# The general path of a fused hash attention and MLP kernel, written as loops over query tiles and row tiles

## The chip, the cores and the metric

The kernel runs on one core of one Trainium2 chip. The metric is device time in microseconds (us); the kernel before was run three times and took 315.37 us in the median (315.19 to 315.73). The profiled execution is a further run of the same kernel.

## What is computed

Attention in which a query sees only those keys that fall in the same hash bucket, then layer norm and a two-layer MLP with a residual.

```python
q_bits = (np.einsum('bhsd,dk->bhsk', q, proj) > 0)      # 6 bits; k_bits alike
mask = q_bucket[:, :, :, None] == k_bucket[:, :, None, :]
scores = scale * np.matmul(q, k.transpose(0, 1, 3, 2))
scores = np.where(mask, scores, -1000000000.0)
scores = scores - np.max(scores, axis=-1, keepdims=True)
attn = np.exp(scores)
attn = attn / (np.sum(attn, axis=-1, keepdims=True) + 1e-09)
x = np.matmul(attn, v)            # then heads side by side: (4, 768, 512)
xn = (x - mu) / np.sqrt(var + 1e-06) * g_ln
out = x + np.maximum(xn @ w_ch1, 0.0) @ w_ch2
```

There are 4 batches, 8 heads, 768 positions and 64 channels a head; q, k and v are normal draws times 0.1. w_ch1 is 512 x 2048, w_ch2 is 2048 x 512.

## The kernel before

The kernel has two paths for the same computation.

**The main path** (all of `tile_hash_attn__then__metaformer_identity_kernel` up to line 901) exponentiates scores without subtracting their maximum first, with the mask folded into the scores as extra rows. It walks through 12 chunks of 256 query rows. For each, attention units (scores on TensorE, the exponential on ScalarE at L456, products with the values at L480) are interleaved with the MLP of the chunk before it (L577 up, L618 and L600 down), by an order written out by hand. The MLP of the last chunk closes the main path: its last row tile is computed in two halves of 256 columns. For each half VectorE adds the residual (L604) and ScalarE's DMA queue stores it (L608). The chunk's other row tile was stored by SyncE's queue (L627).

**The general path** (`general_path`) is exact for scores of any size. It is there for inputs with which the shortcut is not safe. In chunk 10, `safety` computes a flag from the largest squared norms of q and k (L687). After the main path's last work every engine reads that flag into a register (L902) and branches on it (L903): the general path runs when the flag is 0. With these inputs the flag is 1, and no engine runs the general path.

**How the program lies in memory.** Each engine has an instruction stream of its own, in four parts that follow each other: the main path, which ends in the flag's read and the branch; the general path; a short *skip block*, to which the branch goes when the general path isn't wanted; and the *end block*. The skip block exists since the general path would have raised semaphores: each engine waits until its own semaphore has the main path's final value, and then adds what the general path would have added (L903). SyncE does so for those DMA semaphores that the general path uses. The end block (L1080, in the launch code at the file's end) is the same on every run: SyncE waits for 12 semaphores or pairs of them, which cover all DMA queues and all engines; then come a barrier of all five engines, the clearing of the semaphores by GpSimd, and a second barrier. On VectorE the skip block and the end block are six instructions: the semaphore update, a jump, a drain, a wait for the first barrier, a drain, a wait for the second.

SyncE's skip block before has eight semaphore updates, DMAHW0 to DMAHW7, in this order. DMAHW5 and DMAHW6 are the semaphores of the last two stores of the main path (L608). Its twelve waits in the end block name DMAHW5, DMAHW6 and DMAHW7 last.

Of the kernel before, what the change touches and what calls it, by code (L numbers as in the profile page):

```python
# [9 lines left out]
F32 = mybir.dt.float32  # L10
BF16 = mybir.dt.bfloat16
# [897 lines left out]
def general_path(tc, q, k, v, proj1, gbc, n_bits, w1_sb, w2_sb, identf, ident, out):  # L909

    nc = tc.nc
    P = 128
    B, H, S, D = q.shape
    ND, NH = w1_sb.shape[1], w2_sb.shape[1]
    d_model = w2_sb.shape[2]
    NC = S // P
    scale = 1.0 / math.sqrt(D)
    with ExitStack() as ctx:
# [7 lines left out]
        xd = dram.tile([B * H, S, D], F32, name="xd")  # L926
        with tc.For_i(0, B * H, 1) as i:
            nat = {}
            for nm, src in (("q", q), ("k", k), ("v", v)):
                t = pool.tile([P, NC, D], F32, tag=f"g{nm}", name=f"g{nm}")  # L930
                nc.sync.dma_start(
                    out=t,
                    in_=src.rearrange("b h (p c) d -> (b h) p c d", p=P)[
                        bass.ds(i, 1)
                    ].rearrange("o p c d -> (o p) c d"),
                )
                nat[nm] = t
            vb = pool.tile([P, NC, D], BF16, tag="gvb", name="gvb")
            nc.vector.tensor_copy(vb, nat["v"])
            tb, bits = {}, {}  # L940
            for nm in "qk":
                tf = pool.tile([D, S], F32, tag=f"gT{nm}", name=f"gT{nm}")
                for c in range(NC):
                    tp = psp.tile([D, P], F32, tag="gtp", name="gtp")
                    nc.tensor.transpose(tp, nat[nm][:, c, :], identf)
                    nc.vector.tensor_copy(tf[:, c * P : (c + 1) * P], tp)
                tb[nm] = pool.tile([D, S], BF16, tag=f"gb{nm}", name=f"gb{nm}")
                nc.vector.tensor_copy(tb[nm], tf)
                bits[nm] = pool.tile([n_bits, S], BF16, tag=f"gbit{nm}", name=f"gbit{nm}")
                for s0 in range(0, S, S // 2):  # L950
                    hp = psp.tile([n_bits, S // 2], F32, tag="ghp", name="ghp")
                    nc.tensor.matmul(
                        hp, proj1[0:D, 0:n_bits], tf[:, s0 : s0 + S // 2]
                    )
                    nc.vector.tensor_scalar(
                        bits[nm][:, s0 : s0 + S // 2], hp,
                        scalar1=0.0, scalar2=0.5, op0=AOP.is_gt, op1=AOP.subtract,
                    )
            for c in range(NC):
                s = pool.tile([P, S], F32, tag="gs", name="gs")  # L960
                hit = pool.tile([P, S], F32, tag="ghit", name="ghit")
                for s0 in range(0, S, S // 2):
                    sl = slice(s0, s0 + S // 2)
                    bp = psp.tile([P, S // 2], F32, tag="gbp", name="gbp")
                    nc.tensor.matmul(bp, bits["q"][:, c * P : (c + 1) * P], bits["k"][:, sl])

                    nc.vector.tensor_scalar(
                        hit[:, sl], bp, scalar1=n_bits / 4 - 0.25, scalar2=None,
                        op0=AOP.is_gt,
                    )  # L970
                    sp = psp.tile([P, S // 2], F32, tag="gsp", name="gsp")
                    nc.tensor.matmul(sp, tb["q"][:, c * P : (c + 1) * P], tb["k"][:, sl])
                    nc.vector.tensor_scalar_mul(s[:, sl], sp, scale)
                nc.vector.tensor_mul(s, s, hit)
                nc.vector.tensor_scalar(
                    hit, hit, scalar1=1e9, scalar2=1e9, op0=AOP.mult, op1=AOP.subtract
                )
                nc.vector.tensor_add(s, s, hit)
                mx = pool.tile([P, 1], F32, tag="gmx", name="gmx")
                nc.vector.reduce_max(mx, s, axis=AX.X)  # L980
                nc.vector.tensor_scalar(
                    s, s, scalar1=mx, scalar2=None, op0=AOP.subtract
                )
                pb = pool.tile([P, S], BF16, tag="gpb", name="gpb")
                nc.scalar.activation(pb, s, AF.Exp)
                den = pool.tile([P, 1], F32, tag="gden", name="gden")
                nc.vector.reduce_sum(den, pb, axis=AX.X)
                nc.vector.tensor_scalar_add(den, den, 1e-9)
                nc.vector.reciprocal(den, den)
                op = psp.tile([P, D], F32, tag="gop", name="gop")  # L990
                for kj in range(NC):
                    pt_p = psp.tile([P, P], BF16, tag="gpt", name="gpt")
                    nc.tensor.transpose(pt_p, pb[:, kj * P : (kj + 1) * P], ident)
                    pt = pool.tile([P, P], BF16, tag="gpts", name="gpts")
                    nc.vector.tensor_copy(pt, pt_p)
                    nc.tensor.matmul(
                        op, pt, vb[:, kj, :], start=(kj == 0), stop=(kj == NC - 1)
                    )
                xo = pool.tile([P, D], F32, tag="gxo", name="gxo")
                nc.vector.tensor_scalar_mul(xo, op, den)  # L1000
                nc.sync.dma_start(
                    out=xd.rearrange("i (p c) d -> i p c d", p=P)[bass.ds(i, 1), :, c, :]
                    .rearrange("o p d -> (o p) d"),
                    in_=xo,
                )
        xv = xd.rearrange("(b h) (p c) d -> b c p h d", b=B, p=P)
        ov = out.rearrange("b (p c) d -> b c p d", p=P)
        with tc.For_i(0, B, 1) as b:
            for c in range(NC):
                x = pool.tile([P, d_model], F32, tag="gx", name="gx")  # L1010
                nc.sync.dma_start(
                    out=x.rearrange("p (h d) -> p h d", h=H),
                    in_=xv[bass.ds(b, 1), c].rearrange("o p h d -> (o p) h d"),
                )
                stats = pool.tile([P, 6], F32, tag="gst", name="gst")
                mv = pool.tile([P, 2], F32, tag="gmv", name="gmv")
                nc.vector.bn_stats(stats, x)
                nc.vector.bn_aggr(mv, stats)
                rs = pool.tile([P, 1], F32, tag="grs", name="grs")
                mh = pool.tile([P, 1], F32, tag="gmh", name="gmh")  # L1020
                nc.vector.memset(mh, -0.5)
                nc.vector.tensor_scalar_add(rs, mv[:, 1:2], 1e-6)
                nc.gpsimd.tensor_tensor(rs, rs, mh, op=AOP.pow)
                xn = pool.tile([P, d_model], BF16, tag="gxn", name="gxn")
                nc.vector.scalar_tensor_tensor(
                    xn, x, mv[:, 0:1], gbc, op0=AOP.subtract, op1=AOP.mult
                )
                xnT = pool.tile([P, ND, P], BF16, tag="gxnT", name="gxnT")
                for dt in range(ND):
                    tp = psp.tile([P, P], BF16, tag="gpt", name="gxp")  # L1030
                    nc.tensor.transpose(tp, xn[:, dt * P : (dt + 1) * P], ident)
                    nc.vector.tensor_copy(xnT[:, dt, :], tp)
                hb = pool.tile([P, NH, P], BF16, tag="ghb", name="ghb")
                for nt in range(NH):
                    hp = psp.tile([P, P], F32, tag="gsp", name="ghh")
                    for dt in range(ND):
                        nc.tensor.matmul(
                            hp, w1_sb[:, dt, nt * P : (nt + 1) * P], xnT[:, dt, :],
                            start=(dt == 0), stop=(dt == ND - 1),
                        )  # L1040
                    nc.vector.tensor_scalar_max(hb[:, nt, :], hp, 0.0)
                o2 = psp.tile([P, d_model], F32, tag="gop", name="go2")
                for nt in range(NH):
                    nc.tensor.matmul(
                        o2, hb[:, nt, :], w2_sb[:, nt, :],
                        start=(nt == 0), stop=(nt == NH - 1),
                    )
                res = pool.tile([P, d_model], F32, tag="gres", name="gres")
                nc.vector.scalar_tensor_tensor(
                    res, o2, rs, x, op0=AOP.mult, op1=AOP.add  # L1050
                )
                nc.sync.dma_start(
                    out=ov[bass.ds(b, 1), c].rearrange("o p d -> (o p) d"), in_=res
                )


# [28 lines left out]
```

## Time and profile before

| quantity | value |
|---|---|
| median of three runs | 315.37 us (315.19 to 315.73) |
| the profiled execution's own time | 316.02 us |
| its span, from the first to the last instruction of the program | 314.5 us |
| granted TensorE clock over the span | 0.997 |
| TensorE matmuls, busy | 301.7 us (96% of the span) |
| VectorE, ScalarE, GpSimd busy | 185.7, 217.3, 84.4 us |
| HBM traffic | 27.98 MB read, 6.88 MB written |

The profile calls the engines PE (TensorE; PEld are its weight loads), DVE (VectorE), ACT (ScalarE), POOL (GpSimd) and SP (SyncE). A trailing q, as in DVEq, marks instructions that the engine's sequencer carries out itself: branches, semaphore waits and updates, register loads, drains. They are not counted as busy. In the views of one source line a row gives the engine, the instruction, its count, shortest/median/longest duration in ns, and the start of the first and the last in us from the span's start. In the list of DMA queues a row gives packets, megabytes, and the time that the packets took as a share of 16 engines over the window; the queues called "instruction" bring the engines' own code. A row of the table by stretches gives the stretch, its length, each engine's busy time, the granted clock, the share of 16 DMA engines that was busy, and GB/s.

### The profile page before, as it was taken

The numbers are of one execution on the slowest core, as the hardware profiler recorded it, in microseconds if no ns is written. First come the engines' busy times: TensorE is split into PE (matmuls) and PEld (weight loads), VectorE is DVE, ScalarE is ACT, GpSimd is POOL, SyncE is SP. The second block draws the span as 40 slices with busy tenths as digits, with TensorE's granted clock in tenths as the row PEclk, the third lists the DMA queues.
The fourth block names the chain that finished last, engine by engine and source line by source line (L and its number), as shares of the span: only waits on it lengthen the run. The fifth ranks groups of instructions, "written<-read, shape, count | busy, mean of one in ns | idle before, by whom it ended". The sixth has DMA issues, their size and how long they took to land.

```text
span 314.5 us, 7839 instructions
## 1 busy us (share of the span) xinstructions
PE 301.7 (96%) x3268; PEld 226.6 (72%) x3268; DVE 185.7 (59%) x404; ACT 217.3 (69%) x272; POOL 84.4 (27%) x110
## 2 busy tenths in 40 slices
PE   7979999999999999999999999999999999999991
PEld 6556788678679679678678679679688688686661
DVE  1799996653765755744774783743734645456320
ACT  5676977776798778687798777778798577663110
POOL 3467540914320127150470650100100100101000
PEclk9999999999999999999999999999999999999998
DMA  7999998377396467685198655230200210200302
GB/s 249 361 198 302 208 340 121 101 119 186 57 329 136 102 224 139 170 270 142 36 249 157 160 110 120 45 81 2 66 36 2 67 35 2 67 35 2 101 1 76
DMA packets 64971, 40.94 MB, mean 130 GB/s; under 512 B 47153, under 2 KB 59953, under 8 KB 64929
## 3 DMA queue, kind: packets, MB, share of 16 engines
q1 hardware_dynamic: 60224, 31.59, 39.9%
q0 software_dynamic: 4128, 8.13, 11.0%
q10 hardware_dynamic: 576, 0.66, 0.6%
q8 instruction: 27, 0.44, 0.6%
q14 instruction: 16, 0.12, 0.1%
HBM read 27.98 MB, written 6.88 MB: 111 GB/s over the span
## 4 chain that ended last, share of the span: by engine, by line
PE 83%; DVE 10%; ACT 2%; issue 1%; DMA 1%; POOL 0%; ACTq 0%; SPq 0%; POOLq 0%
PE hp L577 25%; PE o L618 23%; PE sc L446 17%; PE av L480 10%; PE hash L321 3%; DVE slots L238 2%; DVE slots L262 2%; PE tpose L200 1%; PE wakep L762 1%; DVE bt L287 1%; PE o L600 1%; PE hash L252 1%; DMA xnT<-xn 1%; DVE xn L529 1%; DVE x L508 1%
## 5 line engine op out<-in xcount | busy, mean ns | idle before, releaser
L456 ACT ACTIVATE ex<-sc,expb 128x1024 bf16<-128x1024 f32 x144 | 159.6, 1113 | 56.5 <-PE sc L446 54.5
L577 PE MATMUL hp<-xnT,w_sb 128*128 128x256 bf16 x768 | 98.7, 272 | 1.7 <-DVE hbuf L587 1.0
L618 PE MATMUL o<-w_sb,hbuf 128*128 128x512 bf16 x368 | 92.9, 379 | 0.0
L446 PE MATMUL sc<-slots 70*128 70x256 bf16 x576 | 86.7, 272 | 2.1 <-POOL slots L238 1.1
L577 PEld LDWEIGHTS <-w_sb 128*128 128x128 bf16 x768 | 72.0, 97 | 11.2 <-issue 2.5
L480 PEld LDWEIGHTS <-ex 128*128 128x128 bf16 x1152 | 54.0, 98 | 15.7 <-ACT ex L456 1.6
L446 PEld LDWEIGHTS <-slots 70*128 70x128 bf16 x576 | 51.8, 97 | 17.5 <-issue 4.5
L480 PE MATMUL av<-vaug,ex 128*128 128x65 bf16 x1152 | 58.8, 194 | 0.3 <-ACT ex L456 0.2
L587 DVE TENSOR_SCALAR hbuf<-hp 128x512 bf16<-128x512 f32 x48 | 32.8, 684 | 43.2 <-PE hp L577 42.0
L618 PEld LDWEIGHTS <-hbuf 128*128 128x128 bf16 x368 | 33.7, 97 | 25.5
L540 POOL TENSOR_SCALAR rs<-mv 128x2 f32<-128x2 f32 x12 | 9.1, 759 | 157.7 <-DVE mv L528 157.7
L589 ACT ACTIVATE hbuf<-hp 128x512 bf16<-128x512 f32 x48 | 28.5, 594 | 20.2 <-PE hp L577 20.2
L623 DVE SCALAR_TENSOR_TENSOR x<-o,rs,x 128x512 f32<-128x512 f32 x23 | 17.1, 744 | 26.3 <-PE o L618 23.4
L529 DVE SCALAR_TENSOR_TENSOR xn<-x,mv,gbc 128x512 bf16<-128x512 f32 x24 | 17.9, 751 | 0.8
L508 DVE TENSOR_TENSOR x<-x,rc 128x256 f32<-128x256 f32 x36 | 17.1, 476 | 1.2
L500 DVE TENSOR_SCALAR rc<-av 128x4 f32<-128x4 f32 x36 | 5.7, 157 | 19.8 <-PE av L480 19.8
L527 DVE BATCH_NORM_STATS2 stats<-x 128x6 f32<-128x512 f32 x24 | 16.5, 690 | 0.4
L351 POOL CAST vaug<-vnat 128x1536 bf16<-128x1536 f32 x8 | 12.1, 1509 | 13.4 <-DMA vnat<-in_v_dram 13.4
L501 DVE TENSOR_TENSOR x<-av,vsum 128x256 f32<-128x256 f32 x36 | 14.9, 414 | 0.0
L180 ACT ACTIVATE knat<-knat 128x768 f32<-128x768 f32 x16 | 13.4, 836 | 0.0
L180 ACT ACTIVATE qnat<-qnat 128x768 f32<-128x768 f32 x16 | 13.3, 833 | 0.0
L282 POOL CAST nat<-qnat 128x1536 bf16<-128x1536 f32 x6 | 8.8, 1470 | 16.7 <-issue 8.7
(86 smaller groups left out, 217.6 us busy)
## 6 DMA issues: line engine op xcount, KB each, us to landing
out_dram<-x SPq DMA_DIRECT2D x23, 256.0 KB
vnat<-in_v_dram SPq DMA_DIRECT2D x7, 768.0 KB
qnat<-in_q_dram SPq DMA_DIRECT2D x11, 384.0 KB
knat<-in_k_dram SPq DMA_DIRECT2D x11, 384.0 KB
w_sb<-in_moe_w_ch_dram POOLq DMA_DIRECT2D x4, 1024.0 KB, 13.8
slots<-slots SPq DMA_DIRECT2D x6, 384.0 KB
qnat<-in_q_dram POOLq DMA_DIRECT2D x2, 768.0 KB, 14.2
knat<-in_k_dram POOLq DMA_DIRECT2D x2, 768.0 KB, 16.3
```

The source lines that it names most:

```text
L180: nc.scalar.activation(src, src, AF.Square, accum_out=sq[:, a, col : col + 1],)
L446: nc.tensor.matmul(sc[:, i, :], key_block(h, kj), query_blocks(h),)
L456: nc.scalar.activation(ex, sc, AF.Exp, bias=expb[:, 1:2] if b else expb[:, 0:1], scale=scale if b else scale / Q_SCALE,)
L480: nc.tensor.matmul(av[:, h - ha, qi, :], state[g][:, i, qi * P : (qi + 1) * P], va[:, h, kj, :], start=(b > 0 and (g, i, qi) == (0, 0, 0)) ...
L508: nc.vector.tensor_tensor(xv, num, rc.unsqueeze(3).to_broadcast([P, 2, TT, D]), op=AOP.mult)
L527: nc.vector.bn_stats(stats, x[:, i, :])
L529: nc.vector.scalar_tensor_tensor(xn[:, :, i, :], x[:, i, :].rearrange("p (o d) -> p o d", d=P), mv[:, i, 0:1], gbc.rearrange("p (o d) -> p ...
L577: nc.tensor.matmul(hp[:, i, :], w1_sb[:, dt, nt * P : (nt + 1) * P], st["xnT"][:, dt, :], start=(dt == 0), stop=(dt == ND - 1),)
L587: nc.vector.tensor_scalar_max(dst, src, 0.0)
L589: nc.scalar.activation(dst, src, AF.Relu)
L618: nc.tensor.matmul(o2, st["h"][:, nt, i * P : (i + 1) * P], w2_sb[:, nt, :], start=(nt == 0), stop=(nt == NH - 1),)
L623: nc.vector.scalar_tensor_tensor(x[:, i, :], o2, st["rs"][:, i : i + 1], x[:, i, :], op0=AOP.mult, op1=AOP.add,)
```

## The change

Only `general_path` is edited. Its loop over the six query tiles of a head becomes a hardware loop inside the loop over heads, and the loop over the six row tiles of a batch becomes one inside the loop over batches. In a hardware loop the query tile can't be picked by a constant slice, so two copies bring it into a small tile. Transposes are gathered: two of q or k, six of the probabilities, four of the normed rows go into one PSUM tile and are copied out together, and four blocks of the MLP's hidden layer share a PSUM tile and one rectifying copy.

```diff
-                for c in range(NC):
-                    tp = psp.tile([D, P], F32, tag="gtp", name="gtp")
-                    nc.tensor.transpose(tp, nat[nm][:, c, :], identf)
-                    nc.vector.tensor_copy(tf[:, c * P : (c + 1) * P], tp)
+                for c in range(0, NC, 2):
+                    tp = psp.tile([D, 2, P], F32, tag="gtp", name="gtp")
+                    for e in range(2):
+                        nc.tensor.transpose(tp[:, e, :], nat[nm][:, c + e, :], identf)
+                    nc.vector.tensor_copy(
+                        tf[:, c * P : (c + 2) * P], tp.rearrange("p e t -> p (e t)")
+                    )
...
-            for c in range(NC):
+            with tc.For_i(0, NC, 1) as c:
+                qc = {}
+                for src in (bits["q"], tb["q"]):
+                    qc[len(qc)] = t = pool.tile(
+                        [src.shape[0], P], BF16, tag=f"gq{len(qc)}", name="gq"
+                    )
+                    nc.vector.tensor_copy(t, src[:, bass.ds(c * P, P)])
...
-                    nc.tensor.matmul(bp, bits["q"][:, c * P : (c + 1) * P], bits["k"][:, sl])
+                    nc.tensor.matmul(bp, qc[0], bits["k"][:, sl])
...
-                    nc.tensor.matmul(sp, tb["q"][:, c * P : (c + 1) * P], tb["k"][:, sl])
+                    nc.tensor.matmul(sp, qc[1], tb["k"][:, sl])
...
+                pt_p = psp.tile([P, NC, P], BF16, tag="gpt", name="gpt")
+                pt = pool.tile([P, NC, P], BF16, tag="gpts", name="gpts")
                 for kj in range(NC):
-                    pt_p = psp.tile([P, P], BF16, tag="gpt", name="gpt")
-                    nc.tensor.transpose(pt_p, pb[:, kj * P : (kj + 1) * P], ident)
-                    pt = pool.tile([P, P], BF16, tag="gpts", name="gpts")
-                    nc.vector.tensor_copy(pt, pt_p)
+                    nc.tensor.transpose(pt_p[:, kj, :], pb[:, kj * P : (kj + 1) * P], ident)
+                nc.vector.tensor_copy(pt, pt_p)
+                for kj in range(NC):
                     nc.tensor.matmul(
-                        op, pt, vb[:, kj, :], start=(kj == 0), stop=(kj == NC - 1)
+                        op, pt[:, kj, :], vb[:, kj, :], start=(kj == 0), stop=(kj == NC - 1)
                     )
...
-            for c in range(NC):
+            with tc.For_i(0, NC, 1) as c:
...
-                for nt in range(NH):
-                    hp = psp.tile([P, P], F32, tag="gsp", name="ghh")
...
+                for n4 in range(0, NH, 4):
+                    hp = psp.tile([P, 4, P], F32, tag="gsp", name="ghh")
```

In the built program the main path is the same, instruction for instruction, on every engine. What differs is the length of the general path, which each engine's branch jumps over, and the skip block. Counted in instructions:

| engine | general path before | after | skip block before | after |
|---|---|---|---|---|
| PE | 1271 | 324 | update, jump | the same |
| DVE | 376 | 150 | update, jump | the same |
| ACT | 63 | 103 | update, jump | the same |
| POOL | 65 | 109 | update, jump | the same |
| SP | 153 | 148 | 8 updates (DMAHW0 to 7), jump | 6 updates (DMAHW0 to 4, and 7), jump |

SyncE's list is shorter since the looped general path issues fewer DMAs, and none on DMAHW5 and DMAHW6. The end block is the same but for the values that it waits for.

More of the change, by code (lines that the diff above doesn't have):

```diff
@@ L1001, in general_path @@
                 nc.sync.dma_start(
-                    out=xd.rearrange("i (p c) d -> i p c d", p=P)[bass.ds(i, 1), :, c, :]
-                    .rearrange("o p d -> (o p) d"),
+                    out=xd.rearrange("i (p c) d -> i p c d", p=P)[bass.ds(i, 1), :, bass.ds(c, 1), :]
+                    .rearrange("o p c d -> (o p) (c d)"),
                     in_=xo,
@@ L1012, in general_path @@
                     out=x.rearrange("p (h d) -> p h d", h=H),
-                    in_=xv[bass.ds(b, 1), c].rearrange("o p h d -> (o p) h d"),
+                    in_=xv[bass.ds(b, 1), bass.ds(c, 1)].rearrange("b c p h d -> (b c p) h d"),
                 )
@@ L1028, in general_path @@
                 xnT = pool.tile([P, ND, P], BF16, tag="gxnT", name="gxnT")
+                tp = psp.tile([P, ND, P], BF16, tag="gpt", name="gxp")
                 for dt in range(ND):
-                    tp = psp.tile([P, P], BF16, tag="gpt", name="gxp")
-                    nc.tensor.transpose(tp, xn[:, dt * P : (dt + 1) * P], ident)
-                    nc.vector.tensor_copy(xnT[:, dt, :], tp)
+                    nc.tensor.transpose(tp[:, dt, :], xn[:, dt * P : (dt + 1) * P], ident)
+                nc.vector.tensor_copy(xnT, tp)
                 hb = pool.tile([P, NH, P], BF16, tag="ghb", name="ghb")
-                for nt in range(NH):
-                    hp = psp.tile([P, P], F32, tag="gsp", name="ghh")
[L1036 to L1041, printed above, removed]
+                for n4 in range(0, NH, 4):
+                    hp = psp.tile([P, 4, P], F32, tag="gsp", name="ghh")
+                    for nt in range(n4, n4 + 4):
+                        for dt in range(ND):
+                            nc.tensor.matmul(
+                                hp[:, nt - n4, :],
+                                w1_sb[:, dt, nt * P : (nt + 1) * P],
+                                xnT[:, dt, :],
+                                start=(dt == 0), stop=(dt == ND - 1),
+                            )
+                    nc.vector.tensor_scalar_max(hb[:, n4 : n4 + 4, :], hp, 0.0)
                 o2 = psp.tile([P, d_model], F32, tag="gop", name="go2")
@@ L1052, in general_path @@
                 nc.sync.dma_start(
-                    out=ov[bass.ds(b, 1), c].rearrange("o p d -> (o p) d"), in_=res
+                    out=ov[bass.ds(b, 1), bass.ds(c, 1)].rearrange("b c p d -> (b c p) d"),
+                    in_=res,
                 )
```

## Prediction

> **What bounds the kernel now.** I read the page's head first, then the chain that ended last over its final 25 us, then the branch and the end, line by line.
>
> ```profile
> span 314.5 us, 7839 instructions
> PE 301.7 (96%) x3268; PEld 226.6 (72%) x3268; DVE 185.7 (59%) x404; ACT 217.3 (69%) x272; POOL 84.4 (27%) x110
> ...
> q8 instruction: 27, 0.44, 0.6%
> q14 instruction: 16, 0.12, 0.1%
> ...
> PE 83%; DVE 10%; ACT 2%; issue 1%; DMA 1%; POOL 0%; ACTq 0%; SPq 0%; POOLq 0%
> ```
>
> TensorE is busy 96% of the span and holds 83% of the chain. No line of `general_path` (L909 on) is among the profile's groups: it isn't run. The diff leaves the main path's instructions as they are, so the 301.7 us of TensorE stay. What can change is what comes after them.
>
> ```profile
> 301.12 3.52 PE o L618 x16
> 304.64 3.51 PE o L600 x32
> 308.15 0.02 issue
> 308.17 0.48 DVE x L604
> ```
>
> The last arithmetic ends at 308.17 + 0.48 = 308.65 us; the span ends at 314.5. These 5.85 us hold the last store, the branch and the end block.
>
> ```profile
> L903 SPq EVENT_SEMAPHORE  x8: 17/17/17, 309.1 to 311.4; - x8
> L903 POOLq COMPARE_BRANCH  x1: 53/53/53, 290.5 to 290.5; - x1
> L903 POOLq EVENT_SEMAPHORE  x1: 17/17/17, 291.1 to 291.1; - x1
> L903 SPq COMPARE_BRANCH  x1: 58/58/58, 306.2 to 306.2; - x1
> L903 PEldq COMPARE_BRANCH  x1: 4002/4002/4002, 306.6 to 306.6; - x1
> L903 DVEq COMPARE_BRANCH  x1: 72/72/72, 308.8 to 308.8; - x1
> L903 ACTq COMPARE_BRANCH  x1: 54/54/54, 309.6 to 309.6; - x1
> L903 ACTq EVENT_SEMAPHORE  x1: 17/17/17, 309.8 to 309.8; - x1
> L903 PEldq EVENT_SEMAPHORE  x1: 51/51/51, 310.7 to 310.7; - x1
> L903 DVEq EVENT_SEMAPHORE  x1: 21/21/21, 311.9 to 311.9; - x1
> ```
>
> From branch to skip block ACT takes 0.2 us and POOL at most 0.6, but SP 2.9, DVE 3.1, PE 4.1. The jumps are 63, 65, 153, 376 and 1271 places long: short ones are free, long ones wait for code. The packets of the instruction queues show it:
>
> ```profile
> 309.60:309.80 0.20, 0.00 (x0) 0.00 (x0) 0.00 (x0) 0.00 (x0) 0.00 (x0) 1.00 1.12 348
> 311.20:311.30 0.10, 0.00 (x0) 0.00 (x0) 0.00 (x0) 0.00 (x0) 0.00 (x0) 1.00 0.69 164
> 311.30:312.40 1.10, 0.00 (x0) 0.00 (x0) 0.00 (x0) 0.00 (x0) 0.00 (x0) 1.00 0.00 0
> 312.50:312.60 0.10, 0.00 (x0) 0.00 (x0) 0.00 (x0) 0.00 (x0) 0.00 (x0) 1.00 0.35 82
> 313.10:314.50 1.40, 0.00 (x0) 0.00 (x0) 0.00 (x0) 0.00 (x0) 0.00 (x0) 0.50 0.00 0
> ...
> q14 instruction: 1, 0.01, 2.3%
> ...
> q8 instruction: 1, 0.02, 10.0%
> ...
> q14 instruction: 1, 0.01, 4.4%
> ...
> q14 instruction: 1, 0.01, 3.5%
> ```
>
> (Rows of the table by stretches, whose last two numbers are DMA share and GB/s; then the instruction rows of the DMA queues for 305.5 to 306.5, 307 to 308, 309 to 310 and 312 to 313 us.) DVE branches at 308.8; a code packet of 4.4% x 16 us = 0.70 us falls in 309 to 310; DVE goes on at 311.9. PE branches at 306.6, its packet of 1.6 us falls in 307 to 308, it goes on at 310.7. Once an engine has landed, the next page of its code follows 0.6 us later: PE's in 311.2 to 311.3, DVE's in 312.5 to 312.6.
>
> The end block says who is last:
>
> ```profile
> L1080 SPq EVENT_SEMAPHORE  x13: 17/28/28, 311.5 to 312.5; - x13
> L1080 SPq DRAIN  x2: 7/10/13, 312.2 to 312.3; - x2
> L1080 POOLq EVENT_SEMAPHORE  x4: 17/17/17, 312.4 to 313.0; - x4
> L1080 ACTq EVENT_SEMAPHORE  x2: 17/17/17, 312.5 to 313.1; - x2
> L1080 DVEq DRAIN  x2: 10/14/17, 312.0 to 312.6; - x2
> L1080 DVEq EVENT_SEMAPHORE  x2: 21/21/21, 312.5 to 314.5; - x2
> L1080 PEldq EVENT_SEMAPHORE  x2: 51/51/51, 312.5 to 313.1; - x2
> SPq L903 <- SPq L903: 4.7, 3, 2.9
> ```
>
> SP reaches the first barrier at 312.3, after DVE (312.0). POOL lets the engines out of the second at 313.0; ACT and PE leave at 313.1, DVE only at 314.5. **DVE's last instruction ends the span 1.4 us after everyone else**, and the only transfer since the first barrier is DVE's code page.
>
> **The change part by part.** *Main path:* the same instructions, nothing added or taken; 0. *Text of the general path:* transposes, copies and loops that aren't run; 0 by themselves. Their count moves the skip and end blocks in the code, which has a price:
>
> *DVE's last wait.* A q14 packet is 0.12 MB / 16 = 7.5 to 8 KB. PE's queue brought 0.44 MB / 27 = 16 KB a packet for 6536 instructions, some 250 a packet, so 64 bytes each (an estimate), and DVE's pages hold 128. The stall before DVE's last instruction puts a page's edge right ahead of it. From the branch that is 1 + 376 + 5 = 382 places, or 3 x 128 - 2: the branch stands at place 2 of a page, the skip block at place 123 two pages on, the last instruction at place 0 of a third. After, the skip block comes 226 places earlier: 2 + 1 + 150 = 153, place 25 of the next page, and the end block ends at place 30. No edge is left in it. Worth 314.5 - 313.1 = **1.4 us**; what is late next are ACT, SP and PE, which leave together.
>
> A rule speaks against this term. The Trainium skill, "Runtime: NRT & Kernel Launch", section "Instruction fetch mechanics", says that crossing into the next block of code is mostly hidden, the sequencer fetching it while it runs the current one. By it DVE's late end would be something else and stay, and the sum would be rival B's. The rows above disagree: the page was asked for only on landing, and DVE had four instructions to hide it behind.
>
> *SP's list.* The second and third of the three waits in SP's row (4.7 - 2.9 = 1.8 us in sum) are for the last two stores; the last store's landing releases SP at 311.4. Then come the update of DMAHW7, the end block's 12 waits and two drains: 15 instructions in 0.9 us (311.4 to 312.3), 0.06 each. After, the skip block no longer names DMAHW5 and 6; the landing is waited for in the end block, with only DMAHW7's wait and two drains behind it: 3 x 0.06. SP reaches the barrier at 311.6 instead of 312.3, **0.7 us** earlier. The other 12 move into time in which SP waited anyway.
>
> *DVE's jump,* the cover of that 0.7: had DVE still come at 312.0, the barrier would stay there. Bounds: 0.2 us (ACT's row) and 3.1 (its own before). After, it goes into the next page, which one q14 packet of 0.37 us (2.3% x 16) brought between 305.5 and 306.5, over 2 us before the branch (no engine had branched to a far place by then but SP, at 306.2). I take 0.2: DVE at the barrier by 309.1. SP's jump of 153 did wait 2.9 us, a row against me; but what counts is pages left behind, and a jump of 153 from the last quarter of a page leaves two edges behind. SP's becomes 148: between 0.2 and 2.9 us, and either way SP's list is through before 311.4, so 0. PE still jumps over at least one whole page (324 places): 4.1 us as now, at 310.7, 0.7 before the landing; 0. ACT (63 to 103) and POOL (65 to 109): a wait of 3 us would bring ACT to 312.6, too late by 1.0; POOL branches 20 us earlier. I take 0: ACT's 103 places are less than a page, so it passes one edge at most, and the page behind one edge is the one that comes ahead of time (+1.0 at worst).
>
> **Sum.** 1.4 + 0.7 = 2.1 us: span 314.5 - 2.1 = 312.4; the profiled execution's 316.02 would be 313.9. Of that 1.5 us lie outside the span; I leave them. The median of the runs is 0.65 below the profiled one: 315.37 - 2.1 = **313.3 us**, 0.7% faster.
>
> **The rivals.**
>
> *B: DVE's late end isn't in the time, or stays.* The 1.5 us outside the span may hide work of the other engines which ends as late as DVE does. Then only SP's 0.7 counts: 314.7. For it: nothing shows what those 1.5 us are. Against: no other engine's code is fetched after 312.6.
>
> *C: every jump out of a page waits for code.* DVE lands at 311.9 as before, SP's wait on DVE's semaphore, now just ahead of the last store's, holds it until then, and 4 x 0.06 brings it to 312.2: the barrier gains 0.1, the end block its 1.4. 315.37 - 1.5 = 313.9. For it: SP's 153. Against: POOL's and ACT's jumps, and the early packet.
>
> *D: nothing.* The general path isn't run, the changed places come out by accident with the same waits, or the time is taken before the end block. 315.4. Against: the edge is exactly where DVE stalls.
>
> *E: an edge in PE's end block: slower.* PE lands at 310.7. If a page of PE's ends between its update and its first drain, PE waits as DVE did, 314.5 - 311.9 = 2.6 us from landing, plus the longer packet (1.6 against 0.56 us): 310.7 + 3.6 = 314.3. From there to ACT's leaving is 313.1 - 312.3 = 0.8: the span ends at 315.1, 0.6 over 314.5, and the time is 316.0. It decides when 1271 - 324 = 947 places fewer put PE's skip block on the last one or two places of a 256-place page. Against: that is 2 places in 256, and PE's branch would have to stand at a place that none of these rows shows.
>
> **How the numbers follow.** Forecast 0.66, B 0.10, C 0.13, D 0.07, E 0.04. The forecast lies at 313.3, with 0.3 to either side from the spread of the three runs (315.19 to 315.73) and 0.1 of rounding: from 312.9. C (313.9) and B (314.7) belong into the range: 312.9 to 314.8. A measurement of this kernel tells 0.2%, 0.63 us, from no change. Forecast, C and B lie beyond it (0.89 faster), D within (0.07), E at its edge (0.04 slower).
>
> **What would show it.** In the profile after: DVE's skip update within 0.3 us of its branch, its last wait together with PE's and ACT's; six SP updates at L903 that end before 310, and one wait for the last store in the end block, at 311.4; span 312.4 with the same 301.7 us of matmuls. No q14 packet in DVE's end block. It is wrong if DVE still leaves last (B), if DVE lands 3 us behind its branch (C), if PE's drain comes behind SP's (E), or if the span falls and the time doesn't.

## The result, and the profile after

| | kernel before | changed kernel |
|---|---|---|
| median of 13 runs each | 315.78 us (315.19 to 316.17) | 313.45 us (312.45 to 315.10) |
| ratio, 95% interval | | 0.993 (0.9916 to 0.9945) |
| profiled execution: time, span | 316.02, 314.5 us | 312.45, 310.6 us |
| time outside the span | 1.5 us | 1.8 us (median of 13) |

The change is 0.7% faster, 2.3 us in the medians; 313.3 was predicted. The profiled execution of the changed kernel is the shortest of its 13, so its span overstates the gain. First the page's head, then the end of the chain of waits:

```profile
span 310.6 us, 7810 instructions
...
PE 299.4 (96%) x3241; PEld 226.0 (73%) x3268; DVE 184.6 (59%) x404; ACT 217.2 (70%) x272; POOL 84.7 (27%) x110
...
q8 instruction: 27, 0.44, 0.6%
q14 instruction: 15, 0.11, 0.1%
```

```profile
303.77 3.51 PE o L600 x32
307.27 0.03 issue
307.30 0.48 DVE x L604
```

The same instructions ran (27 matmul records are missing in this trace, hence 299.4). The last arithmetic ends at 307.78 instead of 308.65: 0.87 us that no edit accounts for. Over all profiles below, with the same main path in each, that moment lies between 306.4 and 310.3; it is the scatter of the main path. Everything after it is counted from that moment from here on.

The branch and the end block of the changed kernel, in the views by source line (L1094 is L1080 of before), and SyncE's waits:

```profile
L903 SPq EVENT_SEMAPHORE  x6: 17/17/17, 308.3 to 308.7; - x6
L903 PEldq COMPARE_BRANCH  x1: 3718/3718/3718, 305.7 to 305.7; - x1
L903 DVEq COMPARE_BRANCH  x1: 72/72/72, 307.9 to 307.9; - x1
L903 DVEq EVENT_SEMAPHORE  x1: 21/21/21, 308.5 to 308.5; - x1
L903 PEldq EVENT_SEMAPHORE  x1: 51/51/51, 309.5 to 309.5; - x1
```

```profile
L1094 SPq DRAIN  x3: 7/7/13, 309.7 to 310.0; - x3
L1094 ACTq EVENT_SEMAPHORE  x2: 17/17/17, 309.9 to 310.5; - x2
L1094 DVEq EVENT_SEMAPHORE  x2: 21/21/21, 310.0 to 310.6; - x2
L1094 PEldq EVENT_SEMAPHORE  x2: 51/51/51, 310.0 to 310.6; - x2
```

```profile
SPq L903 <- SPq L903: 2.9, 1, 2.9
SPq L1094 <- PEq L1094: 0.7, 2, 0.5
SPq L1094 <- PEq L903: 0.2, 1, 0.2
```

VectorE lands, that is, starts its skip block, 0.6 us behind its branch, not 3.1, and leaves the last barrier with ACT and PE, not 1.4 us after them. SyncE's six updates are done by 308.7, and its first drain follows the wait that held it at once. From the last arithmetic to SyncE's first drain it takes 309.7 - 307.8 = 1.9 us, before 312.2 - 308.65 = 3.6; from that drain to the span's end 0.9, before 2.2 (0.9 and VectorE's 1.35; the rows are rounded). In this execution the last wait was for PE's update (the last row), not for the store.

### The profile page after: what moved, and what is told of

Its sections match the earlier page's. It is cut to its first block, busy times and chain, and to the rows that moved or that the text cites. A ratio compares the mean times of both kernels' runs of the same rounds, so it can differ in the third digit from the quotient of the medians.

```text
span 310.6 us, 7810 instructions
## 1 busy us (share of the span) xinstructions
PE 299.4 (96%) x3241; PEld 226.0 (73%) x3268; DVE 184.6 (59%) x404; ACT 217.2 (70%) x272; POOL 84.7 (27%) x110
## 4 chain that ended last, share of the span: by engine, by line
PE 84%; DVE 9%; ACT 3%; issue 2%; DMA 1%; POOL 0%; SPq 0%; ACTq 0%; POOLq 0%
PE hp L577 26%; PE o L618 22%; PE sc L446 18%; PE av L480 10%; PE hash L321 3%; DVE slots L262 2%; PE tpose L200 1%; DVE slots L238 1%; DVE bt L287 1%; PE wakep L762 1%; PE o L600 1%; PE hash L252 1%; DMA xnT<-xn 1%; DVE xn L529 1%; DVE x L508 1%
## 5 line engine op out<-in xcount | busy, mean ns | idle before, releaser
L618 PE MATMUL o<-w_sb,hbuf 128*128 128x512 bf16 x341 | 89.6, 379 | 1.2
```

The costliest lines, as they stand in the source:

```text
L618: nc.tensor.matmul(o2, st["h"][:, nt, i * P : (i + 1) * P], w2_sb[:, nt, :], start=(nt == 0), stop=(nt == NH - 1),)
```

## The experiments

In all kernels below the main path is that of before (in the last three rows the start has a few register moves more or fewer). What is added or left out lies in the general path, which isn't run. Every kernel was timed in five rounds beside the kernel before on the same chip. The table has the time from the last arithmetic to SyncE's first drain and from there to the span's end (both from one profile), the median time outside the span, the median, and the ratio to the kernel before. before_plus8, after_dve376, after_dve248 and after_2dmas ran on one chip; after_again, after_dve385, after_2dmas_b and after_nogeneral on a second; after_c, after_pe1272, after_sp135 and after_nogeneral_b on a third. after_again and after_c are the changed kernel itself.

| kernel | to SP's drain | to the end | outside | median | ratio (95%) |
|---|---|---|---|---|---|
| before | 3.6 | 2.2 | 1.5 | 315.8 to 316.3 | 1 |
| after (first profile) | 1.9 | 0.9 | 1.8 | 313.45 | 0.993 (0.9916 to 0.9945) |
| before_plus8 | 3.5 | 0.9 | 1.8 | 315.03 | 0.9969 (0.9950 to 0.9987) |
| after_dve376 | 3.5 | 0.9 | 2.6 | 315.60 | 1.0002 (0.9980 to 1.0024) |
| after_dve385 | 3.5 | 0.9 | 1.8 | 315.30 | 0.9965 (0.9943 to 0.9987) |
| after_dve248 | 2.8 | 0.9 | 1.8 | 314.24 | 0.9956 (0.9934 to 0.9978) |
| after_2dmas | 3.3 | 0.9 | 1.8 | 314.70 | 0.9961 (0.9938 to 0.9983) |
| after_2dmas_b | 3.5 | 0.9 | 1.8 | 314.83 | 0.9948 (0.9930 to 0.9965) |
| after_again | 2.7 | 0.9 | 1.8 | 314.02 | 0.9921 (0.9899 to 0.9944) |
| after_c | 2.9 | 0.9 | 1.8 | 314.43 | 0.9949 (0.9930 to 0.9968) |
| after_pe1272 | 2.1 | 0.9 | 1.8 | 313.71 | 0.9914 (0.9886 to 0.9943) |
| after_sp135 | 2.7 | 0.9 | 1.5 | 314.40 | 0.9934 (0.9910 to 0.9957) |
| after_nogeneral | 1.9 | 0.9 | 2.0 | 314.03 | 0.9931 (0.9909 to 0.9954) |
| after_nogeneral_b | 1.9 | 0.9 | 2.2 | 313.48 | 0.9926 (0.9900 to 0.9952) |

**The page edge alone: more code, less time.** The kernel before, with

```diff
+        pad = pool.tile([P, 1], F32, tag="gpad", name="gpad")
+        for _ in range(8):
+            nc.vector.memset(pad, 0.0)
         with tc.For_i(0, B * H, 1) as i:
```

> The kernel before, with eight small memsets on VectorE put into the general path, which isn't run. VectorE's branch then jumps 385 places instead of 376, so the page edge should fall ahead of its skip block and no longer ahead of its last instruction. Theory (page edges set the end): VectorE still lands about 3 us behind its branch, SyncE's list and the first barrier stay where they are (312.3 us in the profile), but VectorE leaves the last barrier together with the others: span shorter by 1.35 us, time shorter by 1.0 to 1.4 us, ratio to the kernel before 0.9957 to 0.9968. Rival (the gain comes from a smaller program): nine instructions more, ratio 1.000 or a little above.

VectorE's landing, its end block by source line (L1083 here), and one of SyncE's waits there:

```profile
L903 DVEq COMPARE_BRANCH  x1: 72/72/72, 308.8 to 308.8; - x1
L903 DVEq EVENT_SEMAPHORE  x1: 21/21/21, 311.9 to 311.9; - x1
```

```profile
L1083 SPq DRAIN  x3: 7/7/13, 312.2 to 312.5; - x3
L1083 ACTq EVENT_SEMAPHORE  x2: 17/17/17, 312.4 to 313.0; - x2
L1083 DVEq EVENT_SEMAPHORE  x2: 21/21/21, 312.4 to 313.0; - x2
```

```profile
SPq L1083 <- DVEq L903: 0.6, 1, 0.6
```

VectorE still lands 3.1 us late and SyncE drains at 312.2 as before, but VectorE's last instruction now comes at 313.0 with ACT's. The span is 1.4 us shorter, as the theory has it, and nine instructions more make the kernel 0.8 us faster in the median, a little less than the 1.0 to 1.4 us expected: the rival, a gain from a smaller program, falls. Of the 0.6 us between span and time, 0.3 are in the "outside" column, 1.8 us against 1.5; the rest is within the interval. The 1.5 us that the prediction left alone aren't fixed. The last row says that SyncE waited 0.6 us for VectorE: the store was in earlier here (SyncE's last update at L903 comes at 310.8, before at 311.4), and VectorE's late landing hid it.

**VectorE's old jump in the changed kernel.** 225 and 234 memsets in the same place.

> The changed kernel, with 225 small memsets on VectorE put into the general path, so that VectorE's jump is 376 places again; PE's jump (325) and SyncE's short list stay as in the changed kernel. Theory: VectorE lands 3 us behind its branch and has the edge ahead of its last instruction again, so 1.35 us come back, and with VectorE late at the first barrier most of the 0.75 us of SyncE's list too, and the last store shares a DMA engine with VectorE's code packet again: ratio to the kernel before 0.998 to 1.000. Rival (smaller program, fewer PE instructions): ratio about 0.993 as the changed kernel.

> The changed kernel with 234 small memsets on VectorE in the general path: the jump is 385 places, three pages on as before, but with the edge ahead of the skip block and none in the end block or right behind it. Theory: VectorE lands 3 us behind its branch and holds the first barrier until 3.6 us behind the last arithmetic, as in the kernel before; the late end is gone: 1.0 to 1.2 us faster than before, ratio 0.996 to 0.997, the same as the kernel before with eight memsets; SyncE's short list then brings nothing more. Rival (only the edge counts, VectorE's landing is hidden): ratio 0.993, as the changed kernel.

Landing and leaving of after_dve376 by source line, and the instruction row of its DMA queues for 312 to 314 us, which is after its span of 310.8:

```profile
L903 DVEq COMPARE_BRANCH  x1: 72/72/72, 306.6 to 306.6; - x1
L903 DVEq EVENT_SEMAPHORE  x1: 21/21/21, 309.7 to 309.7; - x1
...
L1097 SPq DRAIN  x3: 7/7/13, 310.0 to 310.3; - x3
L1097 DVEq EVENT_SEMAPHORE  x2: 21/21/21, 310.2 to 310.8; - x2
```

```profile
q14 instruction: 1, 0.01, 1.1%
```

The first has the time of the kernel before, as expected, but not with the late end inside the span: 0.8 us more lie outside it, 2.6 instead of 1.8, and a code packet comes after it. An edge a place or more behind VectorE's last instruction would do that; no row shows the place itself. By the prediction's count both kernels have the edge at the same place, so that count is good to a few places only, and a wait that the span doesn't show still costs.

The second, after_dve385, by source line, with one of SyncE's waits:

```profile
L903 DVEq EVENT_SEMAPHORE  x1: 21/21/21, 313.6 to 313.6; - x1
...
L1097 SPq DRAIN  x3: 7/7/13, 313.8 to 314.1; - x3
...
SPq L1097 <- DVEq L903: 1.8, 1, 1.8
```

It has no late end, and VectorE holds the barrier: SyncE waits 1.8 us for it, 3.5 us pass to SyncE's drain, and the ratio is 0.9965, as in before_plus8 though SyncE's list is short. So SyncE's short list brings nothing unless VectorE lands early.

**The same place with an early landing.** 97 memsets: 128 fewer than in after_dve376, so the same place in a page, one page earlier.

> The changed kernel with 97 small memsets on VectorE in the general path: the jump is 248 places, still into the next page, but the skip block stands at place 123 of it, so the edge is again right ahead of VectorE's last instruction. Theory (the page behind an edge is asked for on landing, 2.55 us before it can be used): VectorE lands early, at about 308.5, so the page is there by about 311.1 and the edge costs little, 0 to 0.5 us over the changed kernel: ratio 0.993 to 0.995. Rival (an edge there costs 1.35 us whatever the landing): ratio about 0.9973.

```profile
L903 DVEq COMPARE_BRANCH  x1: 72/72/72, 309.1 to 309.1; - x1
L903 DVEq EVENT_SEMAPHORE  x1: 21/21/21, 309.6 to 309.6; - x1
...
L1097 DVEq EVENT_SEMAPHORE  x2: 21/21/21, 311.9 to 312.5; - x2
```

VectorE lands 0.6 us behind its branch. The 0.8 us that the same place cost in after_dve376 are gone: 1.8 us outside. In the kernel before the page behind the edge could be used 2.6 us after the landing (311.9 to 314.5); here VectorE's last instruction comes 2.9 us after it (309.6 to 312.5). So an edge cost time in these runs only where the engine had landed less than about 2.6 us before it. The ratio doesn't decide: 0.9956 lies between the theory's 0.995 and the rival's 0.9973, and its interval holds both. The time outside the span does.

**SyncE's list.** Two small loads more in the second loop, so that DMAHW5 and DMAHW6 are in the skip block again:

```diff
+                for e in range(2):
+                    gb = pool.tile([P, 1], F32, tag=f"gex{e}", name="gex")
+                    nc.sync.dma_start(out=gb, in_=q[0, 0, 0:P, e : e + 1])
```

> The changed kernel with two small loads more on SyncE's queue in the second loop of the general path, so that SyncE's skip block names DMAHW5 and DMAHW6 again (eight updates, as before); VectorE's and PE's jumps stay. Theory (12 waits stand behind the last store's landing again): SyncE reaches the first barrier 0.75 us later, ratio to the kernel before about 0.9952, 0.75 us above the changed kernel. Rival (SyncE's list is hidden, another engine is last at the first barrier): ratio 0.993, as the changed kernel.

> The changed kernel once more, beside the next three on one chip. Both theories: ratio to the kernel before 0.992 to 0.995. Its second profile tells how much of the first one's short span is chance: the theory expects DVE's last instruction together with the others', SyncE's drains within 0.25 us of the last wait that holds it, and the time from the last arithmetic to the first barrier anywhere between 2.0 us (no code packet in the way of the last store) and 2.9 us (one in the way).

> The changed kernel with two more loads in the general path once more, beside the changed kernel on one chip: theory 0.75 us above it, rival the same as it.

By source line, after_2dmas_b and then after_again, which ran beside it on one chip, with a row of the latter's waits of SyncE:

```profile
L903 SPq EVENT_SEMAPHORE  x8: 17/17/17, 308.9 to 311.1; - x8
...
L1097 SPq EVENT_SEMAPHORE  x14: 17/28/28, 311.2 to 312.8; - x14
L1097 SPq DRAIN  x3: 7/7/12, 312.0 to 312.3; - x3
```

```profile
L903 SPq EVENT_SEMAPHORE  x6: 17/17/17, 309.4 to 309.8; - x6
...
L1094 SPq EVENT_SEMAPHORE  x14: 17/28/28, 309.9 to 312.4; - x14
L1094 SPq DRAIN  x3: 7/7/13, 311.5 to 311.9; - x3
```

```profile
SPq L1094 <- DMA out_dram<-x: 0.8, 1, 0.8
```

With the long list 0.9 us lie between SyncE's last update (311.1, right behind the store's) and its first drain; in the changed kernel the store's landing is waited for in the end block, and the drain follows 0.1 us behind it (311.41 and 311.55 in the trace). That is the 0.75 us expected. The medians agree, 314.83 against 314.02 us, but the intervals of the two ratios overlap, so the profiles carry this more than the times. after_2dmas, on a chip without the changed kernel, has 3.3 us to the drain and 0.9961. after_again also shows the usual end of the changed kernel: 2.7 us to SyncE's drain, held by the store, where the first profile had 1.9.

**PE's jump.** 474 small matrix products in the general path.

> The changed kernel with 474 small matrix products on PE in the general path, so that PE's jump is 1272 places, as long as before. Theory (PE waits about 4 us for code either way and is 0.6 us ahead of the last store's landing): same as the changed kernel within 0.2 us. Rival (the shorter PE code is where the gain comes from): back towards the kernel before, ratio 0.997 to 1.000.

> The changed kernel a third time, as the reference of the next three on one chip. Both theories: ratio to the kernel before 0.992 to 0.995; first barrier 2.0 to 2.9 us behind the last arithmetic, 2.7 where a code packet stands in the last store's way.

```profile
L903 PEldq COMPARE_BRANCH  x1: 3458/3458/3458, 306.6 to 306.6; - x1
```

With PE's jump as long as before the kernel is no slower than the changed one (0.9914; after_c beside it 0.9949, intervals overlapping), so the rival falls. PE waits 3.5 us at its branch here and 4.0 before, at over 1270 places, and 3.4 to 4.1 us in the profiles with 324 or 325 places: the length of a far jump made no difference.

**What holds up the last store.** In the kernel before, one of the 16 engines moves its share of the last store half a microsecond after the others. Its table by stretches, then that of after_again:

```profile
310.15:310.40 0.25, 0.00 (x0) 0.00 (x0) 0.00 (x0) 0.00 (x0) 0.00 (x0) 1.00 0.00 0
310.40:310.90 0.50, 0.00 (x0) 0.00 (x0) 0.00 (x0) 0.00 (x0) 0.00 (x0) 1.00 0.07 16
310.90:311.20 0.30, 0.00 (x0) 0.00 (x0) 0.00 (x0) 0.00 (x0) 0.00 (x0) 1.00 0.00 0
```

```profile
310.35:310.60 0.25, 0.00 (x0) 0.00 (x0) 0.00 (x0) 0.00 (x0) 0.00 (x0) 1.00 0.00 0
310.60:311.00 0.40, 0.00 (x0) 0.00 (x0) 0.00 (x0) 0.00 (x0) 0.00 (x0) 1.00 0.06 20
```

A share of 0.06 to 0.07 is one engine of 16. These packets begin where a code packet ends (times of single packets, which the trace has finer than the rows): before at 309.71 + 0.70 = 310.41, in after_again at 309.96 + 0.66 = 310.62. The code packet starts 0.56 us after SyncE's landing (309.15, 309.40), so it looks like the page behind that landing. Two tries to take it away:

> The changed kernel with the two DMAs of the second loop of the general path on GpSimd's queue instead of SyncE's (the general path isn't run): SyncE's jump shrinks from 148 places to 135. Theory (the packet that holds up one engine's share of the last store is the page behind SyncE's landing, asked for 0.56 us after a landing that itself waited 2.9 us): SyncE now lands in the next page at once, about 0.2 us behind its branch; its next page comes more than 2 us ahead of the last store; the store lands 1.75 us behind the last arithmetic instead of 2.5, the first barrier comes 0.7 us earlier than in the changed kernel's usual profile; time 0.2 to 0.7 us below the changed kernel on this chip, ratio to the kernel before 0.990 to 0.9925. Rival (SyncE still waits, or another packet takes that place): the same as the changed kernel within 0.2 us.

```diff
-                nc.sync.dma_start(
+                nc.gpsimd.dma_start(
                     out=x.rearrange("p (h d) -> p h d", h=H),
...
-                nc.sync.dma_start(
+                nc.gpsimd.dma_start(
                     out=ov[bass.ds(b, 1), bass.ds(c, 1)].rearrange("b c p d -> (b c p) d"),
```

> The general path is left out of the kernel (a single memset stands in its place), flag, branch and end block stay. All jumps are under five places and SyncE's skip block has no update. Theory: every engine lands within 0.2 us of its branch, no code packet follows the branches, PE is no longer near the end, and the last store's landing alone sets the first barrier, about 2.0 us behind the last arithmetic; ratio 0.990 to 0.9925. Rival (after the change only the store counts, and code packets don't delay it): as the changed kernel on this chip, within 0.2 us.

> The kernel without its general path once more, beside the changed kernel on this chip. Theory: first barrier 2.0 us behind the last arithmetic, 0.7 us less than the changed kernel with a packet in the way; the time outside the span 0.2 us longer, so 0.2 to 0.6 us below the changed kernel. Rival (code packets don't matter to the time): the same within 0.2 us.

SyncE's lines in after_sp135:

```profile
L903 SPq EVENT_SEMAPHORE  x4: 17/17/17, 309.7 to 309.9; - x4
L903 SPq COMPARE_BRANCH  x1: 58/58/58, 306.8 to 306.8; - x1
```

It lands 2.9 us behind its branch as ever: the jump of 135 didn't get SyncE into a page that was there, the try failed at its own first step, and the time is the changed kernel's. Its 1.5 us outside are no gain: its start has four register moves more on GpSimd, and all that follows stands 0.25 us later in the span. Without a general path no engine waits for code, no code packet stands in the store's way, and SyncE drains 1.9 us after the last arithmetic in both profiles. But the time is the changed kernel's on one chip (314.03 and 314.02) and 0.95 us less on the other (313.48 and 314.43); 0.2 to 0.4 us of what the barrier gains are lost again outside the span. That the code packet delays the store fits every profile; what it is worth in time, and what runs outside the span, stays open. No version here beats the changed kernel clearly.

## Why the prediction was right

*That only the end could change:* right. All profiles scatter in the main path, none shows it changed.

*VectorE's last wait, 1.4 us:* right that it goes, and in its size in the span (before_plus8). But the time outside the span grew by 0.3 us, where the prediction left it at 1.5; so the step brought about 1.1 us. The count of places behind it was not exact: after_dve376 has the same count as the kernel before, and no late end inside its span.

The Trainium skill, "Runtime: NRT & Kernel Launch", section "Instruction fetch mechanics", has the crossing into a new block mostly hidden. This case's traces show both: 1.4 us soon after a late landing, no cost seen after an early one (after_dve248).

*SyncE's list, 0.7 us:* right (0.9 us from landing to drain became 0.1), and so is its condition: with VectorE late it brings nothing (after_dve385).

*VectorE's jump, 0.2 us taken:* mis-sized. It took 0.6 us in every kernel with a jump of 150 to 248 places. The packet of 0.70 us that the prediction gave to VectorE's far jump fits SyncE's landing better. VectorE's own is then the one at 310.1 us, 1.3 us behind its branch; after_dve376 and after_dve385 have one at the same distance. Neither changes the sum, since VectorE is 1 to 2 us ahead of SyncE either way.

*PE at 0, SyncE's jump at 0:* right; SyncE's still waits. That PE comes ahead of the store held in the usual profile, by 0.6 us where 0.7 was forecast (310.8 and 311.4 in after_again), not in the first, where the store came early and PE was last.

*The signs:* the common last wait and the six early updates came in the first profile, the store's landing at 311.4 us and the span of 312.4 in after_again. Two came in none. VectorE's update is 0.6 us behind its branch, not within 0.3. And packets of q14 do fall into VectorE's end block, in the first profile two at 309.1 to 309.2; one starts 0.6 us behind VectorE's landing at 308.5, as the prediction's own rows have it for every landing. With no edge there it holds nothing up.

*What the sum lacked:* the landing of the last store moves by up to 1 us between executions (1.9 to 2.9 us to SyncE's drain in the changed kernel's three profiles). Before, VectorE came to the barrier at 312.0, 0.3 us ahead of SyncE, and would have hidden all but 0.3 us of an early store, as it does in before_plus8; now the time follows the store.

So the mechanism is right, and the closeness of the number, 313.45 against 313.3, is in part luck. The kernel before came out 0.4 us slower than the three runs from which the sum starts, the 0.3 us outside the span were not in it, and an earlier store can bring more than it counted. In its two later measurements the changed kernel gained 2.3 and 1.7 us in the medians.

Of the rivals, D and E didn't come, and C is refuted by VectorE's landing 0.6 us behind its branch. Of B the 0.3 us outside the span may be left; what runs there isn't shown.

## What to carry to other kernels

In this case code that never ran had a price, since a branch jumped over it: an engine that landed in a page which wasn't there waited 2.9 to 4.1 us, and one that met a page edge within some 2.6 us of landing waited again. Look at the last branch and the end block of every engine in the views by source line, even where no arithmetic is left. Whatever list stands behind the last store lengthens the end: what can be waited for before that landing should stand before it, provided that no other engine is later still.

## What was not expected

Nine more instructions that aren't run made a kernel 0.3% faster (before_plus8), by moving an edge. A wait can also move out of the span: after_dve376 has a 1.4 us shorter tail in its profile than before and the same time. The time outside the span differed between kernels that differ in code that isn't run: 1.5 us before, 1.8 in most, 2.0 to 2.2 without a general path, 2.6 in after_dve376. Why SyncE waits 2.9 us at jumps of 135 and 148 places, where VectorE waits 0.6 at 150, stays open: the page in which SyncE's branch stands was not found.
